# The last two FFN groups of an attention and FFN kernel: Strassen's scheme on fp32 products, or Karatsuba's on 12-bit halves in float32r

## The chip, the core and the metric

The kernel runs on one core of a Trainium2 chip. The time is that of one execution on the device, in microseconds (us). A core has a matrix engine (TensorE, PE in the profile; its weight loads are PEld), a vector engine (VectorE, DVE), a scalar engine (ScalarE, ACT), a general one (GpSimd, POOL) and a queue for transfers (SyncE, SP). The kernel's matmuls write to PSUM, in tiles of 128 x 512 fp32 that it calls banks; the other operands lie in SBUF.

## What is computed

Threshold attention over 8 sequences of 576 tokens with 8 heads of 64, then an FFN with ELU over the 4608 tokens, all in fp32:

```python
scores = scale * np.matmul(q, k.transpose(0, 1, 3, 2))
thresh = np.max(scores, axis=-1, keepdims=True) - tau
scores = np.where(scores >= thresh, scores, -1000000000.0)
attn = np.exp(scores - max); attn = attn / (sum + 1e-09)     # over the last axis
x = np.matmul(attn, v)                                       # (4608, 512)
h = x @ w_in                                                 # (4608, 2048)
g = np.where(h > 0.0, h, np.exp(np.minimum(h, 0.0)) - 1.0)
out = g @ w_out                                              # (4608, 512)
```

## The kernel before

The FFN works on groups of 512 tokens. Group 0 is done with plain products (`ffn1`, `ffn2_plain`), the others as told here. Group 0 to 7 are the first 512 tokens of each sequence; the 64 tokens left of each sequence make group 8. `xts[g]` holds a group's tokens turned, as four slices `j` of 128 channels; for group 8 they are collected in DRAM (`xtail`) as each sequence is finished, and the part of the last sequence's last head pair comes last.

The attention runs a head pair at a time. From the second sequence on, its steps (`wide_step`, `tail_step`) and the FFN of an earlier sequence share TensorE: after each half step the loop at L1954 lets `ffn_quarters` run a number of quarters of FFN products. The order on each engine is written out: `on_pe` moves a clock by a planned cost for each piece of matmul work, and `at` puts the work of the other engines on an agenda at planned times; the agenda's order is the order in which the engines' queues get their instructions. On the chip the queues run in that order as soon as what each instruction waits for is there.

A group is done by Strassen's scheme with seven products in place of eight. `first_product(g, u)` (L1643) makes one of eight units of the hidden layer: seven products (`left`, `right` at L1660) of two matmuls each with 256 columns, accumulated in three PSUM banks, their sums taken apart by ACT copies, POOL and DVE additions (`after_` at L1720), then exp, minus one and a maximum (`exp`, `minus`, `elu`). `sums` (L1738) makes the sums of the hidden layer that the second product needs; `second_round(g, r)` (L1774) does the output product in two rounds, each with two chunks of 256 tokens, seven products of four matmuls each (L1804). The sums of the weights are made early in the kernel, kept in DRAM (`win_sums`, `wout_sums`) and loaded by SP when they are due (`next_in`, `next_t`); parts of `w_in_sb` and `w_out_sb` in SBUF are replaced by differences (`change_in`, `change_out`).

Groups 1 to 6 run this way between attention steps. After the last attention step (`pr == NP + 1`), where the values of the last head pair are made and copied to `xts[7]`, sums of group 7's tokens are taken (`sums_x`, L1270) and groups 7 and 8 follow with nothing else on TensorE; their order is the list at L2032. The loop at L2005 and L2036 places the remaining sums.

Of the kernel before, what the change touches and what calls it, by code (L numbers as in the profile page):

```python
# [10 lines left out]
FP32 = mybir.dt.float32  # L11
U32 = mybir.dt.uint32
I32 = mybir.dt.int32
AF = mybir.ActivationFunctionType
# [353 lines left out]
def kernel(  # L368
# [33 lines left out]
    raw = ctx.enter_context(tc.tile_pool(name="raw", bufs=1))  # L402
    qkp = ctx.enter_context(tc.tile_pool(name="qkp", bufs=2))
    att = ctx.enter_context(tc.tile_pool(name="att", bufs=2))
    small = ctx.enter_context(tc.tile_pool(name="small", bufs=4))
    wtp = ctx.enter_context(tc.tile_pool(name="wtp", bufs=1))
    xpool = ctx.enter_context(tc.tile_pool(name="xpool", bufs=2))
    gpool = ctx.enter_context(tc.tile_pool(name="gpool", bufs=1))
    epool = ctx.enter_context(tc.tile_pool(name="epool", bufs=1))
# [28 lines left out]
    w_in_sb = const.tile([P, KJ, DF], FP32, name="w_in_sb")  # L438
# [13 lines left out]
    pieces = [(moe_w_in, w_in_sb[:, j, n : n + WN], j, n) for n in range(0, DF, WN) for j in range(KJ)]  # L452
# [86 lines left out]
    def load_v(pr):  # L539
        b, j = divmod(pr, NPAIR)  # L540
        tiles = raws[pr]
        vm = tiles["vm"] = (wstage if pr < 2 else raw).tile([P, 2, NC, D], FP32, name="vm", bufs=2)
# [304 lines left out]
    def turn_squares(pr, i):  # L847
        w = open_steps.pop((pr, i))["w"]
        if late:
            x = late["x"].tile([P, NT, NCH, T], FP32, name="x", bufs=2)  # L850
        else:
            x = wstage.tile([P, 2 * S + TAIL], FP32, name="x", bufs=2)[:, : NT * NCH * T]
            x = x.rearrange("p (g c n) -> p g c n", c=NCH, n=T)
# [189 lines left out]
    def values_out(pr, part, pv):  # L1043
# [5 lines left out]
        if part:  # L1049
            xs = epool.tile([P, TAIL], FP32, name="xs", bufs=2)  # L1050
# [28 lines left out]
    def ffn1(c, u):  # L1079
# [4 lines left out]
        def part(x):  # L1084
# [4 lines left out]
            for j in range(j0, j0 + 2):  # L1089
                nc.tensor.matmul(loc["ph"][:, k], w_in_sb[:, j, ft * P : (ft + 1) * P],  # L1090
# [46 lines left out]
    def ffn2_plain(c, i, part):  # L1137
# [7 lines left out]
        def done():  # L1145
            ot = epool.tile([P, DM], FP32, name="ot", bufs=4)
# [63 lines left out]
    def blocks_in(u):  # L1210
        f0, f1 = (slice(f * P, (f + 1) * P) for f in (u, NU + u))
        return w_in_sb[:, :2, f0], w_in_sb[:, 2:, f0], w_in_sb[:, :2, f1], w_in_sb[:, 2:, f1]

    def room_in(u):
# [3 lines left out]
        sw = late["x"].tile([P, 3, 2, P], FP32, name="sw", bufs=2)  # L1218
# [77 lines left out]
    def early_tasks():  # L1296
# [35 lines left out]
        def leave_early():  # L1332
            early.close()
            late["x"] = wpool[0] = ctx.enter_context(tc.tile_pool(name="late", bufs=1))
# [121 lines left out]
        for n in range(MIDDLE):  # L1456
# [103 lines left out]
            if n >= SWITCH:  # L1560
# [9 lines left out]
                if n >= MIDDLE - 2:  # L1570
                    def some(x):
                        if "jobs" not in late:
                            late["jobs"] = sums_x(1, [late["x"].tile([P, 2, CT], FP32, name=f"x{z}") for z in range(3)])
# [27 lines left out]
    with tc.manual_schedule():  # L1601
# [39 lines left out]
        first_order = [(g, u) for g in range(1, B + 1) for u in range(NU)]  # L1641
# [435 lines left out]
```

## Time and profile before

| | us |
|---|---|
| median of 3 runs | 1278.2 (1277.52 to 1280.78) |
| span of the profiled execution, first to last instruction | 1275.5 |
| of it up to 1055 | 1055.0: PE busy 1045.5, DVE 893.3, ACT 553.0, POOL 697.5 |
| most of group 6's last second round | 1055.0 to 1071.6 |
| the last attention step on TensorE | 1071.6 to 1077.3: PE busy 5.25, DVE 2.65, ACT 1.05, POOL 0 |
| groups 7 and 8 | 1077.3 to 1271.6 |
| the last additions and the store | 1271.6 to 1275.5 |

Of the profiled execution the trace holds the span; it lies 2.7 us under the median. Times in rows of the timeline are us from the start of the span; the first number is the start, the second the length. `x8` stands for eight records in a row. A matmul's length in the trace is modelled and overlaps the next, so its rate is read from starts. A row of a source line gives min, median and max in ns, then the first and last start.

### The profile page before, as it was taken

The page shows a single profiled execution, that of the slowest core. Times are in us where ns is not written, and L with a number is a line of the kernel's source. Part 1 is how long each engine was busy: PE and PEld are TensorE (multiplying, and loading weights), DVE is VectorE, ACT ScalarE, POOL GpSimd, SP SyncE. Part 2 cuts the span into 40 slices and gives each one's busy share as a digit, 9 for nine tenths or more (in the row PEclk, how much of TensorE's full clock was granted, in tenths as well). Part 3 has the DMA queues.
Part 4 walks back from the last instruction along what each step waited for, and adds up shares of the span by engine and source line. Part 5 has one row for each costly group of instructions (what it writes and reads, how often), then busy time and mean ns, then how long its engine had stood idle before and what let it go on. Part 6 is the DMA issues. An engine that isn't in the chain of part 4 may idle for free.

```text
span 1275.5 us, 21472 instructions
## 1 busy us (share of the span) xinstructions
PE 1261.3 (99%) x6726; PEld 983.8 (77%) x6726; DVE 994.8 (78%) x2142; ACT 606.7 (48%) x1309; POOL 789.2 (62%) x1141
## 2 busy tenths in 40 slices
PE   8999999999999999999999999999999999999998
PEld 6675575467778887878888877878887888888887
DVE  7888877888889979898889888988989772544534
ACT  7899776664443535252625353443535251421320
POOL 4778665786585748584766657675757473534533
PEclk9999999999999999999999999999999999999999
DMA  7467688997988998999889998988898874122211
GB/s 141 150 170 190 169 244 236 259 278 200 251 217 241 252 239 228 252 262 229 232 233 269 225 256 205 263 225 243 214 268 232 241 229 177 53 77 73 83 62 34
DMA packets 329586, 258.35 MB, mean 203 GB/s; under 512 B 209536, under 2 KB 290432, under 8 KB 329472
## 3 DMA queue, kind: packets, MB, share of 16 engines
q1 hardware_dynamic: 327376, 256.50, 73.7%
q8 instruction: 53, 0.87, 0.3%
q10 hardware_dynamic: 2096, 0.48, 0.2%
q14 instruction: 61, 0.50, 0.1%
HBM read 167.12 MB, written 89.78 MB: 201 GB/s over the span
## 4 chain that ended last, share of the span: by engine, by line
PE 91%; DVE 3%; DMA 2%; ACT 1%; issue 1%; SPq 1%; POOL 1%; DVEq 0%; ACTq 0%; POOLq 0%
PE f L1804 30%; PE f L1664 29%; PE sc L965 8%; PE sc L1038 7%; PE f L1090 4%; PE sc L661 3%; PE f L1142 3%; PE pv L918 2%; PE rt L780 1%; PE sc L1030 1%; PE sc L1025 1%; DMA there<-x 1%; PE pv L913 1%; DVE x L856 1%; DMA qm<-in_q_dram 0%
## 5 line engine op out<-in xcount | busy, mean ns | idle before, releaser
L972 DVE TENSOR_REDUCE mx<-sc 128x1 f32<-128x576 f32 x207 | 148.2, 750 | 29.5 <-PE sc L965 25.6
L714 POOL TENSOR_SCALAR w<-w,rs 128x576 f32<-128x576 f32 x144 | 115.8, 812 | 70.8 <-DVE rs L777 70.1
L992 ACT ACTIVATE w<-sc,mx 128x576 f32<-128x576 f32 x113 | 81.4, 739 | 115.0 <-DVE mx L972 98.0
L1664 PE MATMUL f<-xt,sw 128*128 128x256 f32 x512 | 124.0, 385 | 1.1 <-ACT g L1726 0.5
L1664 PE MATMUL f<-xt,w_in_sb 128*128 128x256 f32 x512 | 122.2, 381 | 0.5 <-ACT w L1678 0.5
L856 DVE STREAM_TRANSPOSE x<-w 128x512 f32<-128x512 f32 (+1 forms) x153 | 108.9, 744 | 13.0 <-POOL w L714 11.2
L984 POOL TENSOR_SCALAR th<-mx,ntau 128x2 f32<-128x2 f32 (+1 forms) x114 | 33.8, 296 | 133.3 <-DVE mx L972 133.2
L1664 PEld LDWEIGHTS f<-xt,sw 128*128 128x128 f32 x512 | 93.5, 190 | 21.5 <-issue 4.5
L1664 PEld LDWEIGHTS f<-xt,w_in_sb 128*128 128x128 f32 x512 | 96.2, 190 | 16.1 <-ACT w L1678 3.1
L1804 PE MATMUL f<-w_out_sb,g 128*128 128x256 f32 x448 | 107.1, 382 | 0.0
L1804 PE MATMUL f<-w_out_sb,s 128*128 128x256 f32 x448 | 107.0, 382 | 0.0
L1664 PE MATMUL f<-x,w_in_sb 128*128 128x256 f32 x448 | 105.9, 379 | 0.0
L1804 PE MATMUL f<-t,s 128*128 128x256 f32 x448 | 105.8, 379 | 0.0
L965 PE MATMUL sc<-kT,qT 64*128 64x448 f32 (+4 forms) x736 | 102.7, 416 | 0.0
L965 PEld LDWEIGHTS sc<-kT,qT 64*128 64x128 f32 x736 | 80.9, 186 | 24.4 <-issue 16.2
L1751 POOL TENSOR_TENSOR s<-g 128x256 f32<-128x256 f32 x104 | 80.5, 780 | 27.4 <-PE f L1804 20.1
L999 DVE SCALAR_TENSOR_TENSOR w<-sc,th,w 128x576 f32<-128x576 f32 x113 | 88.2, 810 | 9.5 <-ACT w L992 9.2
L1804 PEld LDWEIGHTS f<-w_out_sb,g 128*128 128x128 f32 x448 | 84.1, 190 | 14.2 <-issue 3.2
L1804 PEld LDWEIGHTS f<-w_out_sb,s 128*128 128x128 f32 x448 | 84.1, 190 | 13.6 <-issue 2.5
L1664 PEld LDWEIGHTS f<-x,w_in_sb 128*128 128x128 f32 x448 | 85.0, 190 | 11.8 <-ACT s L1678 0.3
L1804 PEld LDWEIGHTS f<-t,s 128*128 128x128 f32 x448 | 85.1, 190 | 11.6
L714 POOL TENSOR_SCALAR e<-e,rs 128x576 f32<-128x576 f32 x91 | 67.0, 740 | 35.3 <-DVE rs L777 33.9
(233 smaller groups left out, 2858.7 us busy)
## 6 DMA issues: line engine op xcount, KB each, us to landing
there<-x SPq DMA_DIRECT2D x444, 144.0 KB, 3.5
wTb<-there SPq DMA_DIRECT2D x58, 576.0 KB, 6.3
wTa<-there SPq DMA_DIRECT2D x53, 576.0 KB, 4.9
sw<-win_sums SPq DMA_DIRECT2D x62, 384.0 KB, 4.0
t<-wout_sums SPq DMA_DIRECT2D x45, 512.0 KB, 5.5
qm<-in_q_dram SPq DMA_DIRECT2D x124, 72.0 KB, 4.8
wst<-in_moe_w_in_dram SPq DMA_DIRECT2D x16, 512.0 KB, 4.4
vm<-in_v_dram SPq DMA_DIRECT2D x64, 128.0 KB, 3.5
```

Of the source, the lines that this page charges most:

```text
L661: nc.tensor.matmul(scs[h][:, a, :HALF], qs[r], kT[r, k0 : k0 + HALF], start=True, stop=True)
L714: nc.gpsimd.tensor_scalar(wv, wv, st["rs"][:, h : h + 1], 1.0, ALU.mult, ALU.mult)
L856: nc.vector.transpose(x[:, :, c0 : c0 + nc_], src.rearrange("p (c g n) -> p g c n", c=nc_, n=T))
L965: on_banks(nc.tensor.matmul(o, qT[r, i * P : (i + 1) * P], kT[r, k0 : k0 + n], start=True, stop=True, skip_group_check=True), o)
L972: on_banks(nc.vector.tensor_reduce(st["mx"][:, h : h + 1], st["sc", h], axis=AX.XY if i == NC else AX.X, op=ALU.max, negate=True), st["sc" ...
L992: on_banks(nc.scalar.activation(st["e", h], st["sc", h], AF.Exp, bias=st["mx"][:, h : h + 1]), st["sc", h])
L999: on_banks(nc.vector.scalar_tensor_tensor(st["e", h], st["sc", h], st["th"][:, h : h + 1], st["e", h], ALU.is_ge, ALU.mult, accum_out=st[" ...
L1038: on_banks(nc.tensor.matmul(o, vm[:, h, c], parts[part][:, g0:g1, h * (NC + 1) + c], start=False, stop=(c == NC - 1), skip_group_check=Tru ...
L1090: nc.tensor.matmul(loc["ph"][:, k], w_in_sb[:, j, ft * P : (ft + 1) * P], xts[g][:, j, hf * CT : (hf + 1) * CT], start=(j == 0), stop=(j = ...
L1664: nc.tensor.matmul(loc["banks"][place], left[:, j], right[:, j], start=(begins and j == 0), stop=(j == 1), skip_group_check=True)
L1751: engine.tensor_tensor(o, x, y, op)
L1804: nc.tensor.matmul(place(m), lhs, rhs, start=(begins and v == 0), stop=(v == RU - 1), skip_group_check=True)
```

## The change

Up to group 6 every engine's instructions stay as they are, in the same order (some tiles lie elsewhere: pools are opened so that the attention's memory and Strassen's can be given back early; `w_in_sb` becomes two tiles, `w_in_lo` and `w_in_hi`). Groups 7 and 8 are done anew.

Every operand v is cut in two: a = v x (1 - 2^-13), rounded on writing to the 4-byte type float32r, and the rest b = v - a. With a third operand made of both, three products a·a', b·(b' scaled) and a cross product give the whole. For a weight: `weights_cut` (ACT), `weights_rest` (POOL), `weights_scaled` (ACT), `weights_cross` (DVE). For tokens and for the hidden layer: `cut` (ACT), `rest` (DVE or POOL), `cross` (DVE). Each works on 128 x 512. Before weights can be cut, the differences in them are undone (`restore_in` on DVE, `restore_out` on POOL, 256 columns each).

`split_begin` starts this 13 us after the beginning of the step `pr == NP`, while group 6's last second round still runs: it gives back the attention's memory, loads group 8's tokens, and cuts three slices of group 7's tokens, two weight blocks and two slices of group 8. The rest follows in the new stage. First product: 32 units (one block of 128 hidden channels of one group each), of 12 matmuls of 512 columns: the first five are of group 7, then blocks of group 8 and group 7 come mostly in turn; ACT scales the PSUM bank between the first eight and the last four. Second product: for each group 16 blocks, for each block four tiles of 128 tokens with three matmuls of 512 columns. The first three and the last three blocks are ordered by tile, so that these six are wanted together.

```diff
+        def cut(key, src, cols=slice(0, DM), fresh=True):
+            a = take(key, F32R) if fresh else parts[key][0][0]
+            nc.scalar.activation(a[:, cols], src()[:, cols], AF.Copy, scale=CUT)
+        def rest(key, src, engine, cols=slice(0, DM), fresh=True):
+            b = take(key, F32R) if fresh else parts[key][1][0]
+            engine.tensor_tensor(b[:, cols], src()[:, cols], parts[key][0][0].bitcast(FP32)[:, cols], ALU.subtract)
+        def cross(key, src, cols=slice(0, DM), fresh=True):
+            s = take(key, F32R) if fresh else parts[key][2][0]
+            nc.vector.scalar_tensor_tensor(s[:, cols], parts[key][0][0].bitcast(FP32)[:, cols], 1.0 + EPS, src()[:, cols],
+                                           ALU.mult, ALU.subtract)
+        def split_tokens(t, key, src, engine):
+            at(t, lambda: cut(key, src))
+            at(t + 0.8, lambda: rest(key, src, engine))
+            at(t + (0.8 if engine is nc.gpsimd else 1.5), lambda: cross(key, src))
...
+        def weights_rest(key, src, engine):
+            d = slot(FP32)
+            parts["d", key] = [d]
+            engine.tensor_tensor(like(d[0], src()), src(), like(parts[key][0][0].bitcast(FP32), src()), ALU.subtract)
+        def weights_scaled(key):
+            nc.scalar.activation(take(key, F32R), parts["d", key][0][0], AF.Copy, scale=1.0 / EPS)
+        def weights_cross(key):
+            nc.vector.scalar_tensor_tensor(take(key, F32R), parts["d", key][0][0], 1.0 / EPS,
+                                           parts[key][0][0].bitcast(FP32), ALU.mult, ALU.subtract)
+            drop(("d", key))
...
+        def split_weights(t, key, src, engine):
+            at(t, lambda: weights_cut(key, src))
+            at(t + 0.7, lambda: weights_rest(key, src, engine))
+            end = t + (2.3 if engine is nc.gpsimd else 1.6)
+            at(end, lambda: weights_scaled(key))
+            at(end + 0.1, lambda: weights_cross(key))
...
+        def split_begin():
+            t = now[0]
+            attention.close()
+            open_slots("r", 24, "right")
+            xts[B] = xpool.tile([P, KJ, MAIN], FP32, name="xt")
+            nc.sync.dma_start(xts[B][:, : KJ - 1], xtail[: KJ - 1].rearrange("j p n -> p j n"))
+            nc.sync.dma_start(xts[B][:, KJ - 1, : late_columns.start], xtail[KJ - 1, :, : late_columns.start])
+            for j in range(KJ - 1):
+                split_tokens(t + 0.2 + 2.2 * j, ("x", B - 1, j), x_of(B - 1, j), nc.vector)
+            for f in range(2):
+                at(t + 6.6 + 3.0 * f, lambda f=f: restore_in(f))
+                split_weights(t + 7.2 + 3.0 * f, ("in", f), w_in_of(f), nc.gpsimd)
+            for j in range(2):
+                split_tokens(t + 13.0 + 2.4 * j, ("x", B, j), x_of(B, j), nc.vector)
...
+            if pr == NP:
+                at(t + 13.0, split_begin)
...
+        UNIT, ONE = 2.58, 0.215
+        order = [(g7, f) for f in range(5)]
...
+        split_tokens(begin + 1.0, ("x", g8, 2), x_of(g8, 2), nc.gpsimd)
+        split_tokens(begin + 6.0, ("x", g8, last), x_of(g8, last), nc.vector)
+        for f in range(2, NFT):
+            t = max(begin + 1.5 + 2.6 * (f - 2), start_of[g7, f] - 7.0)
+            at(t - 0.6 if f < NU else begin + 2.0 + 2.5 * (f - NU), lambda f=f: restore_in(f))
+            split_weights(t, ("in", f), w_in_of(f), nc.gpsimd)
+        for u in range(NU):
+            at(begin + 30.0 + 5.0 * u, lambda u=u: restore_out(u))
...
+        def first_round(n, js):
+                    nc.tensor.matmul(o, w.rearrange("p (j f) -> p j f", j=KJ)[:, j], m, start=(j == 0 and x == 0),
+                                     stop=(j == KJ - 1 and x == 1), skip_group_check=True)
+        def cross_round(n):
...
+            at(t + 0.05, exp)
+            at(t + 0.85, minus)
+            at(t + 1.65, elu)
...
+        for f in range(NFT):
+            lead = 9.0 - 1.2 * min(f, EDGE - 1) if f < EDGE else 6.5
+            t = start_f(middle, f) - lead + 1.5 * min(f, EDGE) * (f < EDGE)
+            split_weights(t, ("out", f), w_out_of(f), nc.gpsimd)
+            split_g(t + 0.6, g7, f, nc.vector)
+            t = start_f(end, f) - (9.0 if f < EDGE else 6.5) + 1.5 * f * (f < EDGE)
+            at(t + 1.0, lambda f=f: nc.vector.tensor_tensor(take(("cross", f), F32R), parts["out", f][1][0].bitcast(FP32),
+                                                            parts["out", f][0][0].bitcast(FP32), ALU.subtract))
+            split_g(t, g8, f, nc.gpsimd if f % 2 else nc.vector)
+        def second(g, f, i):
+            tok = slice(i * P, (i + 1) * P)
+            for x in range(3):
+                h = issued(("h", g, f), x)
+                w = issued(("out", f), x) if x < 2 or g == g7 else issued(("cross", f), 0)
+                nc.tensor.matmul(banks8[2 * i + x // 2], h[:, tok], w, start=(f == 0 and x != 1),
+                                 stop=(f == NFT - 1 and x != 0), skip_group_check=True)
...
+            if f == NFT - 1:
...
+                    at(t + 0.05 + 0.4 * x, lambda cols=cols: nc.scalar.activation(
+                        o[:, cols], banks8[2 * i][:, cols], AF.Copy, scale=1.0 + EPS))
+                    at(t + (0.5 if done else 0.8) + 0.45 * x, lambda cols=cols: nc.vector.tensor_tensor(
+                        o[:, cols], banks8[2 * i + 1][:, cols], o[:, cols], ALU.add))
```

`EDGE` is 3, `EPS` 2^-12 and `CUT` 1 - 2^-13; `begin`, `middle` and `end` are the planned starts of the stage and of the second products of groups 7 and 8. Slots for the cut operands are two pools of 24 and 34 tiles of 128 x 512.

276 lines of the change are left out of this document (197 added, 79 removed).

## The prediction

> **What bounds the kernel now.** I read the page's totals and its chain of waits first, then the windows, then the order of time on TensorE at the end.
>
> ```profile
> span 1275.5 us, 21472 instructions
> PE 1261.3 (99%) x6726; PEld 983.8 (77%) x6726; DVE 994.8 (78%) x2142; ACT 606.7 (48%) x1309; POOL 789.2 (62%) x1141
> PE 91%; DVE 3%; DMA 2%; ACT 1%; issue 1%; SPq 1%; POOL 1%; DVEq 0%; ACTq 0%; POOLq 0%
> ```
>
> TensorE is busy 99% of the span and 91% of the chain that ended last is TensorE. Nothing else can shorten the kernel but less array work. The instructions of every engine stand in the same order in both programs until the last second round of group 6, so only the end matters; the windows split it (after the length: busy us of PE, PEld, DVE, ACT, POOL).
>
> ```profile
> 1055.00:1071.60 16.60, 16.60 (x78) 14.36 (x76) 3.64 (x9) 0.37 (x1) 9.71 (x14) 1.00 0.28 103
> 1077.30:1174.40 97.10, 97.08 (x450) 85.48 (x451) 51.05 (x88) 29.14 (x69) 43.88 (x58) 1.00 0.23 78
> 1174.40:1271.60 97.20, 96.74 (x448) 84.56 (x446) 43.67 (x82) 23.17 (x55) 38.06 (x51) 1.00 0.20 62
> 1271.60:1275.50 3.90, 0.10 (x1) 0.00 (x0) 0.53 (x2) 0.00 (x0) 0.00 (x0) 0.83 0.30 67
> ```
>
> Groups 7 and 8 fill 1077.3 to 1271.6, TensorE without gaps, the other engines at most half used. The clock is 1.00. The time per instruction comes from starts in the timeline:
>
> ```profile
> 1077.32 1.99 PE L1664 MATMUL f<-xt,sw 128*128 128x256 f32 x8 [0.47 <-ACT xt L1048]
> 1079.15 1.03 PE L1664 MATMUL f<-x,sw 128*128 128x256 f32 x4
> 1080.02 1.89 PE L1664 MATMUL f<-xt,w_in_sb 128*128 128x256 f32 x8
> 1081.74 1.89 PE L1664 MATMUL f<-x,w_in_sb 128*128 128x256 f32 x8
> ...
> 1254.17 1.99 PE L1804 MATMUL f<-w_out_sb,qm 128*128 128x256 f32 x8 [0.46 <-DVE ot L1824]
> 1256.00 1.89 PE L1804 MATMUL f<-w_out_sb,wTa 128*128 128x256 f32 x8
> ...
> 1269.81 1.89 PE L1804 MATMUL f<-w_out_sb,x 128*128 128x256 f32 x8
> L1804 PEld LDWEIGHTS f<-w_out_sb,g 128*128 128x128 f32 x448 | 84.1, 190 | 14.2 <-issue 3.2
> ```
>
> From 1256.00 to 1269.81 are eight rows of x8, 64 records in 13.81 us: 0.2158 each. An fp32 matmul of the program leaves two records (a product of four matmuls shows as x8): 0.4316 us for 256 columns. The weight load of 190 ns hides under each record. 448 matmuls of the two groups are 896 records, 193.4 us; with the waits of 0.47 and 0.46 that is the stage.
>
> **The array work.** The new scheme has 2 groups x (16 blocks x 12 + 16 blocks x 4 token tiles x 3) = 768 matmuls of 512 columns in float32r. No row shows this type. In fp32 256 columns cost four passes of 0.108 us; if one-pass means what it says, 512 columns cost 0.2158, and the 190 ns load still fits under it. For the bound from above, fp32 records of 512 columns:
>
> ```profile
> L1142 PE MATMUL f<-w_out_sb,g 128*128 128x512 f32 x128 | 60.1, 602 | 0.0
> ```
>
> They last 602 ns where those of 256 columns in the page's list last 379 to 385: a record streams 256 columns in 0.22, so one record of 512 would take 0.43. From below, a matmul bound by its weight load would take 0.19. I take 0.2158, as a single pass is what the type is for and two would be odd with both halves gone: 768 x 0.2158 = 165.7, minus 27.7 us. The Trainium skill (FP8 and Floating Point Precision, TensorE Precision Notes) tells of a reduced mode that reads 4-byte values and truncates them, against four passes for true fp32, and names no rate; no run here shows it. The skill's TensorE: Matmul & The Clock Gate (Wait — 56ns, not 53.3ns?) has 215.7 ns for a one-pass matmul of 512 columns in bf16, which would make 165.7 as well. The two old waits go too (minus 0.9).
>
> **What it adds.** Every operand is now cut on chip: ACT cuts, POOL or DVE subtracts, ACT or DVE makes the third operand. Their prices:
>
> ```profile
> L1273 DVE TENSOR_TENSOR x<-xt x19: 672/681/710, 258.1 to 1077.3; 128x512 f32<-128x512 f32 x19
> L1751 DVE TENSOR_TENSOR s<-s,g x8: 415/422/426, 1094.4 to 1212.1; 128x256 f32<-128x256 f32 x8
> L1255 POOL TENSOR_TENSOR t<-w_out_sb x4: 1262/1270/1273, 209.0 to 232.4; 128x512 f32<-128x512 f32 x4
> L1234 POOL TENSOR_TENSOR w_in_sb<-w_in_sb x8: 726/730/1177, 239.1 to 260.5; 128x256 f32<-128x256 f32 x8
> L1704 POOL TENSOR_SCALAR ge<-ge x54: 612/618/831, 273.3 to 1248.3; 128x512 f32<-128x512 f32 x54
> L1694 ACT ACTIVATE ge<-g x77: 612/630/636, 272.3 to 1198.5; 128x512 f32<-128x512 f32 x77
> L1097 ACT ACTIVATE g<-f x16: 574/590/599, 60.7 to 207.8; 128x512 f32<-128x512 f32 x16
> L1104 DVE SCALAR_TENSOR_TENSOR g<-g,f x13: 667/680/689, 63.5 to 209.1; 128x512 f32<-128x512 f32 x13
> L1714 DVE SCALAR_TENSOR_TENSOR g<-ge,g x77: 660/771/1208, 274.6 to 1199.9; 128x512 f32<-128x512 f32 x77
> ```
>
> So 512 columns cost 0.68 on DVE, 1.27 on POOL (subtract) or 0.62 (scalar), 0.63 on ACT; a restore of 256 columns 0.42 on DVE, 0.73 on POOL. Alone each engine has room in 2.58 us, TensorE's time for one block (12 x 0.2158 = 2.59): in group 7's second product DVE needs 3 x 0.68 = 2.04, POOL 1.27, ACT 3 x 0.63 = 1.89; in the first product ACT has scale and exp 2 x 0.59 and two weight steps 2 x 0.63 = 2.44 in the first five units. But the maximum of L1714, 1208 ns, shows that they are not alone:
>
> ```profile
> 1104.31 0.72 POOL L1683 TENSOR_TENSOR u<-u,w 128x256 f32<-128x256 f32 x1
> 1104.37 1.21 DVE L1714 SCALAR_TENSOR_TENSOR g<-ge,g 128x512 f32<-128x512 f32 x1 [0.51 <-POOL ge L1704]
> 1105.11 1.06 POOL L1683 TENSOR_TENSOR s<-s,u 128x256 f32<-128x256 f32 x1
> 1109.39 0.61 POOL L1704 TENSOR_SCALAR ge<-ge 128x512 f32<-128x512 f32 x1
> 1109.45 1.08 DVE L1714 SCALAR_TENSOR_TENSOR wTb<-km,wTb 128x512 f32<-128x512 f32 x1 [0.51 <-POOL km L1704]
> ```
>
> DVE ends 0.55 after POOL's end at 1105.03, POOL's next then 0.59 after DVE's at 1105.58; at 1110.00 the same, 0.53. An instruction of DVE with two SBUF inputs and one of POOL run in turn; a waiting one hides some 0.13 of its own time. L1104, with one input in PSUM, never stretches. Every split on DVE has two SBUF inputs, so DVE and POOL times **add**. Three places follow, each bounded by full prices and by prices less 0.13.
>
> *Before the stage* (1055 to 1071.6, 16.6 us): POOL has 9.7 already; the change puts in five token splits (10 x 0.68), two weight blocks (2 x 1.27 + 2 x 0.68) and two restores (2 x 0.42): 21.2, 4.6 too much; with 0.13 off each of 30 instructions, 17.3, 0.7 too much. The second block's subtract stands on POOL ahead of the sums of chunk 1 that TensorE needs
>
> ```profile
> 1064.35 1.41 POOL L1751 TENSOR_TENSOR s<-g 128x256 f32<-128x256 f32 x2
> 1066.36 1.89 PE L1804 MATMUL f<-t,s 128*128 128x256 f32 x8
> ```
>
> only 0.6 us after they are made, and waits itself for DVE's restore and ACT's cut. So I take 3.5.
>
> *The start of the first product*: five units of group 7 come in a row, each with a new weight block. Until TensorE wants block 4 (4 x 2.58 = 10.3 us) the pair has: POOL four subtracts (5.1) and two scalars (1.2); DVE four half splits (1.7), three splits of group 8 (2.0), two weight crosses (1.4), seven restores (2.9): 14.3, 4.0 over; less 0.13 for each of 22, 11.4, 1.1 over. Queues here mix restores for later blocks ahead of what is urgent: 3.5. Later blocks come every second unit (5.2 us). The other 27 units, 69.7 us of matmuls, hide what the pair still has (27 scalars, 11 subtracts, 12 crosses, 7 restores on DVE and 8 on POOL: 48 us): nothing, and at most those 48 without the cover.
>
> *Group 7's second product*: a block costs the pair 1.27 + 3 x 0.68 = 3.31 against 2.58. From the first subtract, 8.3 us ahead of the product by the queue's plan, to the last three blocks, wanted together 33.5 us into it, are 41.8 us; 16 blocks and three scalars are 54.9, 13.1 over; less 0.13 for each of 67, 46.2, 4.4 over. As the two engines wait for each other all the time here, the low end is nearer: 6. Group 8 reuses the weights: 0.68 + 0.68 and 0.68 or 1.27 are 2.34 a block on average, 37 us under 41 of matmuls: nothing (the 37 would show if DVE started late). ACT's share is hidden everywhere by those same matmuls; its thinnest cover is 0.14 us a unit, in the first five.
>
> The Trainium skill (SBUF — State Buffer, Who interferes with whom) says that these two kinds of instruction exclude each other for a whole instruction; it speaks against this change. By that rule to the letter the three waits are the upper ends, 4.6, 4.0 and 13.1, and the time 1271.8; the rows above agree but for the 0.13 that overlap.
>
> *The end*: the last tile needs ACT's scale (0.37 for half) ahead of DVE's add: +0.5 (0 to 1). The loads of Strassen's sums go and two loads of tokens come; TensorE waits for no DMA in this stage (share 0.20 to 0.28), so both at nothing.
>
> Sum: -27.7 - 0.9 + 3.5 + 3.5 + 6 + 0.5 = -15.1. The profiled span of 1275.5 lies 2.7 under the median of 1278.2, and that stays around it: 1260.4 of span, **1263 us**. With the lower ends of the waits (0.7, 1.1, 4.4, 0) 1255.8, with the upper ones 1272.3.
>
> **Rivals.** (1) The pair's blocking costs nothing, since queues run ahead; for it: POOL was 39 to 45% busy here; against: 1208 ns at L1714. What is left is the chain: a subtract of 1.27 and a sum of 0.72 against 0.6 of slack, 1.4, and as much at the start: -28.6 + 2.8 + 0.5, 1253. (2) The pair is worse than full prices, as no instruction arrives in time and each restarts a chain cut, subtract, scale (0.63 + 1.27 + 0.63): another 3 to 6 on the upper ends, 1275 to 1278. (3) float32r is not one-pass but streams like one fp32 record, 0.43: 768 x 0.43 = 330, plus 137, all splits hidden: 1414, **slower**; it decides from 0.25 us a matmul. Against it: nothing would be gained by the type. (4) In group 7's second product weight and token chains run one block at a time, for want of slots: cut, subtract, scale, cross 3.2 and token 2.0 make 5.2 a block, (5.2 - 2.58) x 16 = 42 in place of 6: 1299, slower; it decides from 3.8 a block. Against it: 58 slots of 512 columns stand open.
>
> **Chances.** Forecast (1256 to 1272) 0.62; (1) 0.10; (2) 0.15; (3) 0.06; (4) 0.05; the rest 0.02. A measurement of this kernel tells 0.3%, some 3.8 us, from no change: (2) lies half there. Faster 0.82, same 0.06, slower 0.12. The range of 1253 to 1277 leaves out 0.2.
>
> **What would show it.** The new profile should have about 768 matmul records starting 0.216 apart; DVE groups at the subtract and cross lines with means well over 0.68 and POOL subtracts over 1.27; gaps on TensorE released by POOL ahead of the stage, by ACT in the first 13 us of it, by DVE in group 7's second product and none in group 8's. Matmuls 0.43 apart, or means at 0.68 beside gaps, would make it wrong.

## The result, and the profile after

| | before | after |
|---|---|---|
| median | 1278.2 us (9 runs, 1277.05 to 1280.78) | 1274.72 us (9 runs, 1273.13 to 1276.79) |
| span of the profiled execution | 1275.5 | 1271.7 |

The ratio is 0.9969, 95% interval 0.9959 to 0.9979: faster by 3.5 us, where 15 were forecast. The time lies above the upper end of the range, 1272. The page of the changed kernel, totals and chain of waits:

```profile
span 1271.7 us, 21210 instructions
PE 1246.8 (98%) x6598; PEld 957.3 (75%) x6598; DVE 1035.4 (81%) x2146; ACT 651.2 (51%) x1363; POOL 804.6 (63%) x1114
PE 87%; DVE 5%; issue 2%; DMA 2%; ACT 2%; POOL 1%; SPq 1%; ACTq 0%; DVEq 0%; POOLq 0%
```

TensorE still bounds it. It is busy 14.5 us less than before, but its share of the chain falls from 91% to 87%: there are waits now. The windows of the changed kernel (after the length: PE, PEld, DVE, ACT, POOL, then the clock and the DMA share):

```profile
1048.24:1077.19 28.95, 25.72 (x114) 20.70 (x112) 15.42 (x24) 6.25 (x12) 17.78 (x19) 1.00 0.42 148
...
1098.26:1173.51 75.25, 75.25 (x334) 62.33 (x332) 33.62 (x50) 46.82 (x87) 42.84 (x50) 1.00 0.00 1
1173.51:1217.00 43.49, 40.31 (x168) 32.18 (x167) 43.49 (x50) 24.54 (x44) 25.80 (x16) 0.96 0.00 1
...
1210.60:1217.00 6.40, 3.93 (x11) 2.81 (x10) 6.40 (x12) 2.18 (x4) 2.19 (x1) 0.73 0.00 0
...
1213.51:1216.92 3.41, 3.41 (x8) 2.74 (x9) 3.41 (x6) 1.66 (x3) 2.11 (x1) 0.50 0.00 0
...
1217.00:1266.88 49.88, 49.88 (x219) 40.71 (x217) 34.57 (x44) 10.59 (x20) 13.47 (x8) 1.00 0.10 32
```

Group 6's last second round takes 28.95 and has gaps; the first product after its fifth unit and group 8's second product have none; in group 7's second product DVE is busy for every one of 43.49 us and TensorE is not. The rate and the gaps are in the timeline:

```profile
1068.39 0.41 DVE L2055 TENSOR_TENSOR w_in_lo<-w_in_lo,w_in_hi 128x256 f32<-128x256 f32 x1
1068.84 0.63 ACT L2021 ACTIVATE r<-w_in_lo 128x512 fp32r<-128x512 f32 x1 [0.94 <-DVE w_in_lo L2055]
1069.55 1.26 POOL L2026 TENSOR_TENSOR r<-w_in_lo,r 128x512 f32<-128x512 f32 x1 [1.62 <-ACT r L2021]
1070.77 1.86 POOL L1762 TENSOR_TENSOR s<-g 128x256 f32<-128x256 f32 x2
1071.55 2.26 PE L1815 MATMUL f<-t,s 128*128 128x256 f32 x8 [2.88 <-POOL s L1762]
...
1083.88 1.35 POOL L2001 TENSOR_TENSOR l<-xt,l 128x512 fp32r<-128x512 f32 x1 [7.08 <-ACT l L1997]
1085.19 1.47 POOL L2026 TENSOR_TENSOR l<-w_in_lo,l 128x512 f32<-128x512 f32 x1
1086.14 0.39 PE L2182 MATMUL f<-r,l 128*128 128x512 f32 x1
1086.86 0.63 ACT L2029 ACTIVATE l<-l 128x512 fp32r<-128x512 f32 x1
1087.54 1.88 PE L2182 MATMUL f<-r,l 128*128 128x512 f32 x7 [1.01 <-ACT l L2029]
...
1098.26 1.07 PE L2182 MATMUL f<-r,r 128*128 128x512 f32 x4
1099.16 1.07 PE L2182 MATMUL f<-l,r 128*128 128x512 f32 x4
1100.07 1.07 PE L2195 MATMUL f<-r,l 128*128 128x512 f32 x4
...
1190.34 0.39 PE L2261 MATMUL f<-w_in_hi,l 128*128 128x512 f32 x1
...
1191.04 0.39 PE L2261 MATMUL f<-w_in_hi,r 128*128 128x512 f32 x1
...
1195.28 0.68 DVE L2001 TENSOR_TENSOR r<-w_in_lo,l 128x512 fp32r<-128x512 f32 x1
1195.89 0.68 DVE L2005 SCALAR_TENSOR_TENSOR r<-l,w_in_lo 128x512 fp32r<-128x512 f32 x1
1196.08 1.64 POOL L2026 TENSOR_TENSOR l<-w_out_sb,w_in_hi 128x512 f32<-128x512 f32 x1 [1.27 <-ACT w_in_hi L2021]
1196.49 1.78 DVE L2032 SCALAR_TENSOR_TENSOR r<-r,w_in_hi 128x512 fp32r<-128x512 f32 x1
1198.19 0.68 DVE L2001 TENSOR_TENSOR r<-w_in_lo,r 128x512 fp32r<-128x512 f32 x1
...
1213.46 0.78 PE L2261 MATMUL f<-r,l 128*128 128x512 f32 x1 [2.47 <-DVE r L2032]
1214.04 0.63 PE L2261 MATMUL f<-r,r 128*128 128x512 f32 x1
```

Four things are to be seen. (a) 1098.26 to 1100.07 are eight matmuls in 1.81 us: 0.2267 each, not 0.2158; 1190.34 to 1191.04, where every third streams `w_in_hi`, are three in 0.70 (two rows between are left out): 0.231 to 0.233. (b) The 2.88 us ahead of the stage wait for a sum on POOL, behind the subtract of 1069.55, which waited for a cut on ACT, which waited for a restore on DVE. (c) At the start of the first product TensorE waits for ACT's scaled weights, three times about alike. (d) DVE needs 1195.28 to 1198.19, 2.91 us, for each block of group 7's second product, of which the weight cross takes 1.70, since POOL's subtract runs in between; at 1213.46 TensorE has waited 2.47 us, and the matmuls behind it start 0.43 to 0.58 apart: the clock granted was half for 3.41 us (0.50 in the window from 1213.51, 0.73 on average in the one from 1210.60).

A step is the time from the start of one matmul to the start of the next. With the starts of the first matmuls of each stretch in both traces, the 3.8 us of span come out like this:

| term | forecast | measured | how |
|---|---|---|---|
| all up to group 6's last second round | 0 | +1.0 | its first matmul at 1047.26 and 1048.24; 0.85 of it is there from 258 us on, for a reason that was not traced |
| that round | +3.5 | +4.6 | 24.37 and 28.95 from its first matmul to the attention step's |
| array work | -27.7 | -18.2 | 193.4, and 175.2 = stage of 184.5 less its waits of 9.35 (next three rows) |
| waits at the start | +3.5 | +4.0 | steps over 0.26 between starts, up to 1096, less 0.2267 each |
| waits in group 7's second product | +6 | +3.6 | the same at 1175.1 and 1210.6 |
| matmuls at half clock behind the gap | - | +1.7 | eight steps, 1213.46 to 1217.0, in 3.53 |
| old waits | -0.9 | -1.4 | 0.83 in the old stage, 0.54 ahead of it |
| end, behind the last matmul | +0.5 | +0.9 | 3.96 and 4.86 |
| sum | -15.1 | -3.8 | |

768 matmuls in 175.2 us are 0.2281 each. That one term holds 9.5 of the 11.3 us by which the sum is off.

### The profile page after: what moved, and what is told of

It is laid out like the page before. It is cut to its first block, busy times and chain, and to the rows that moved or that the text cites. A ratio compares the mean times of both kernels' runs of the same rounds, so it can differ in the third digit from the quotient of the medians.

```text
span 1271.7 us, 21210 instructions
## 1 busy us (share of the span) xinstructions
PE 1246.8 (98%) x6598; PEld 957.3 (75%) x6598; DVE 1035.4 (81%) x2146; ACT 651.2 (51%) x1363; POOL 804.6 (63%) x1114
## 4 chain that ended last, share of the span: by engine, by line
PE 87%; DVE 5%; issue 2%; DMA 2%; ACT 2%; POOL 1%; SPq 1%; ACTq 0%; DVEq 0%; POOLq 0%
PE f L1815 22%; PE f L1675 22%; PE sc L974 8%; PE sc L1047 7%; PE f L2182 4%; PE f L1099 4%; PE f L2261 4%; PE sc L670 3%; PE f L1151 3%; PE pv L927 2%; PE f L2195 2%; PE rt L789 1%; PE sc L1039 1%; PE sc L1034 1%; DMA there<-x 1%
## 5 line engine op out<-in xcount | busy, mean ns | idle before, releaser
L981 DVE TENSOR_REDUCE mx<-sc 128x1 f32<-128x576 f32 x207 | 148.3, 750 | 29.2 <-PE sc L974 25.2
L865 DVE STREAM_TRANSPOSE x<-w 128x512 f32<-128x512 f32 (+1 forms) x153 | 108.9, 744 | 14.0 <-POOL w L723 11.3
L1815 PE MATMUL f<-t,s 128*128 128x256 f32 x384 | 91.7, 380 | 3.2 <-POOL s L1762 3.1
L1675 PE MATMUL f<-xt,sw 128*128 128x256 f32 x384 | 93.6, 386 | 0.7 <-ACT g L1737 0.5
L1815 PE MATMUL f<-w_out_sb,g 128*128 128x256 f32 x384 | 92.0, 382 | 0.0
L1815 PE MATMUL f<-w_out_sb,s 128*128 128x256 f32 x384 | 91.9, 382 | 0.0
L1815 PEld LDWEIGHTS f<-t,s 128*128 128x128 f32 x384 | 72.5, 190 | 14.9 <-POOL s L1762 5.2
L1675 PEld LDWEIGHTS f<-xt,sw 128*128 128x128 f32 x384 | 69.3, 189 | 17.3 <-issue 5.0
L1001 ACT ACTIVATE e<-sc,mx 128x576 f32<-128x576 f32 x91 | 66.5, 744 | 24.6 <-DVE mx L981 23.2
L1008 DVE SCALAR_TENSOR_TENSOR e<-sc,th,e 128x576 f32<-128x576 f32 x91 | 71.2, 810 | 7.6 <-ACT e L1001 7.6
L865 DVE STREAM_TRANSPOSE x<-e 128x640 f32<-128x640 f32 x92 | 66.0, 755 | 1.0
L727 DVE TENSOR_REDUCE mx<-sc 128x1 f32<-128x576 f32 x81 | 59.3, 747 | 5.5 <-PE sc L670 5.1
```

What stands on the lines that cost most here:

```text
L727: nc.vector.tensor_reduce(st["mx"][:, h : h + 1], st[h][:, :, :HALF], axis=AX.XY, op=ALU.max, negate=True)
L865: nc.vector.transpose(x[:, :, c0 : c0 + nc_], src.rearrange("p (c g n) -> p g c n", c=nc_, n=T))
L981: on_banks(nc.vector.tensor_reduce(st["mx"][:, h : h + 1], st["sc", h], axis=AX.XY if i == NC else AX.X, op=ALU.max, negate=True), st["sc" ...
L1001: on_banks(nc.scalar.activation(st["e", h], st["sc", h], AF.Exp, bias=st["mx"][:, h : h + 1]), st["sc", h])
L1008: on_banks(nc.vector.scalar_tensor_tensor(st["e", h], st["sc", h], st["th"][:, h : h + 1], st["e", h], ALU.is_ge, ALU.mult, accum_out=st[" ...
L1675: nc.tensor.matmul(loc["banks"][place], left[:, j], right[:, j], start=(begins and j == 0), stop=(j == 1), skip_group_check=True)
```

## The experiments

Differences are to the changed kernel's 1274.72 unless said otherwise; ratios are to the kernel before, measured beside it.

**What a float32r matmul costs.** Behind the last store, rows of 16 matmuls on idle engines (`w` and `m` lie like the slots, `hi` is `w_in_hi`, `half` bf16, `full` fp32):

```diff
         until(1e9)
+        hi = parts["c"][0]
...
+        kinds = (lambda k: (cut4(w, k), m), lambda k: (w[:, :P], m), lambda k: (cut4(w, k, 64), m),
+                 lambda k: (cut4(w, k, 32), m), lambda k: (cut4(w, k, 32), m[:, :384]), lambda k: (cut4(w, k, 32), m[:, :CT]),
+                 lambda k: (cut4(w, k), m[:, :CT]), lambda k: (cut4(half[1], k), half[0]),
+                 lambda k: (cut4(full, k), full[:, :CT]), lambda k: (cut4(w, k), hi[:, 1]),
...
+                nc.tensor.matmul(o[: st.shape[1], : mv.shape[1]], st, mv, start=k == 0, stop=k == 15, skip_group_check=True)
```

> After the last store the changed kernel is followed by 19 rows of 16 matmuls each on otherwise idle engines, so only the rows' spacing matters, not the time. In the stage float32r matmuls of 512 columns start 0.2267 us apart, and 0.231 apart while a slice of w_in_hi streams, where fp32 records start 0.2158 apart. Theory A (a fixed extra of some 0.011 per float32r matmul, whatever its widths): 512 columns stay at 0.227 with 128, 64 or 32 stationary columns; with 32 stationary columns 384 columns take 0.173 and 256 columns 0.119. Theory B (the 4-byte weight load of 0.19 isn't wholly hidden): 0.227 with 128 stationary columns falls to 0.216 with 64 and 32; 256 columns with 128 stationary ones stay near 0.2. Theory C (the moving operand streams a sixteenth slower): 0.227 for any stationary width, 384 columns 0.170, 256 columns 0.113. Theory D (the other engines disturb it): 0.216 in the first row, since nothing else runs. The same stationary block sixteen times: 0.227 for A and C; for B as well, unless a repeated load is left out. bf16 of 512 columns and fp32 records of 256: 0.216 for all. For w_in_hi (it lies elsewhere in SBUF than the slots, and on a multiple of 64 bytes, the slots 32 off): if place or alignment decides, 0.23 or more for rows that stream w_in_hi, and, if alignment, for the row that starts 32 bytes into a slot as well.

Windows of this run, TensorE alone, each from the first start of a kind to that of the next. In order: 64 and 32 stationary columns; 32 with 384 and with 256 moving columns; bf16 (15 recorded); fp32 of 256 columns (31 steps); the moving operand 0 and 32 bytes into a slot; both operands in `w_in_hi`; moving in a slot, stationary in `w_in_hi`:

```profile
1279.38:1283.05 3.67, 3.67 (x17) 1.00 0.00 0
1283.05:1286.76 3.71, 3.71 (x17) 1.00 0.00 0
1286.76:1289.54 2.78, 2.78 (x18) 1.00 0.00 0
1289.54:1291.42 1.88, 1.88 (x17) 1.00 0.00 0
...
1293.57:1296.81 3.24, 3.24 (x16) 1.00 0.00 0
1296.81:1303.50 6.69, 6.69 (x32) 1.00 0.01 2
1314.85:1318.48 3.63, 3.63 (x18) 1.00 0.00 0
...
1322.19:1325.92 3.73, 3.73 (x17) 1.00 0.00 0
...
1329.59:1333.24 3.65, 3.65 (x17) 1.00 0.00 0
1333.24:1336.98 3.74, 3.74 (x18) 1.00 0.00 0
```

Divided by 16: 0.229 and 0.232 with narrow weights, so the weight load isn't it (B); 0.174 for 384 and 0.1175 for 256 columns, which is 0.162 and 0.108 (512 columns of 0.2158, in proportion) plus 0.012 and 0.010: a fixed extra (A), and no slower streaming, which would give 0.170 and 0.113 (C); with 128 stationary columns 256 columns take 0.120, 0.012 over too. A expected 0.227 with narrow weights too; that they come out 0.002 to 0.005 above it is not explained. The other engines are idle here, so they aren't it (D). bf16 at 3.24 / 15 and fp32 at 6.69 / 31 keep 0.216: the extra belongs to float32r. Place matters too: 0.2267 where both operands lie alike, 0.234 for one in `w_in_hi` and one in a slot, but 0.2267 again (the last steps of that row) with both in `w_in_hi`, and 0.233 for 32 bytes into a slot. It is their difference that costs.

**Equal remainders, first try.** In the compiled program `w_in_hi` starts at a remainder of 64 by 128 bytes, the slots at 96. A pad ahead of each pool of slots makes all 64:

```diff
+            pad = split_stack.enter_context(tc.tile_pool(name=name + "_pad", bufs=1, side=side))
+            pad.tile([P, 8 if name == "r" else 24], FP32, name=name + "_pad")
             pool = split_stack.enter_context(tc.tile_pool(name=name, bufs=1, side=side, reuse_waits="tile"))
```

> Changed kernel, with a pad of 32 and of 96 bytes ahead of the two pools of slots, so that slots and w_in_hi start at the same remainder by 128 bytes. Theory A (a float32r matmul costs 0.227 where both operands start at the same remainder, 0.231 to 0.234 where not, and in the second products every third matmul streams w_in_hi): all undisturbed matmuls of both second products start 0.2267 apart, the mean outside the waits falls from 0.2282 to 0.227, 0.9 us less of stage. Theory B (w_in_hi is slower for its place in SBUF): 0.231 stays and so does the stage. The time of one look can't tell 0.9 us.

A miss for both: the mean step outside the waits rose from 0.2282 to 0.2316, and in the first product alone from 0.2270 to 0.2317. By 256 bytes the two pools now stood at 192 and 64, where they had been 224 both. So 128 is the wrong measure.

**By offset.** Rows of 24, the moving operand off by a number of bytes:

```diff
+        for b in (0, 4, 8, 12, 16, 24, 32, 40, 48, 64, 80, 96, 112, 128, 256, 512):
+            rows(w, m, 0, b)
```

> Again rows of matmuls behind the changed kernel, 24 each, on idle engines: float32r of 512 columns with the moving operand 0, 16, 32, 48, 64, 96, 128, 160, 192, 256, 320, 384, 448, 512, 1024 and 2048 bytes off the stationary one's remainder by 512; then both shifted by 32 bytes, both by 256, the stationary one 512 and the moving one 256 on; then bf16 and fp32 with the operands 0 and 32 bytes apart. So far: 0.2267 apart at equal remainders, 0.2294 to 0.2335 at 16 to 160 bytes of difference, and 0.231 in the run with slots at remainders of 448 and 64 by 512. Theory A (equal remainders by 512 bytes cost the fixed extra of 0.011 alone, others 0.003 to 0.007 more; the extra itself isn't a matter of place): 0.2267 for 0, 512, 1024, 2048 and for both shifted, more for all others, none under 0.2265. Theory B (the extra is itself a clash of the streamed operand with the next weight load, which some difference avoids): a row at 0.216. For bf16 and fp32 records 0.216 with equal remainders; at 32 bytes apart 0.216 if the clash belongs to float32r, more if it doesn't.

Windows of this run, 24 steps each: 32 bytes off, 160, 256, 512, and bf16 32 bytes off:

```profile
1284.45:1290.04 5.59, 5.59 (x25) 1.00 0.00 0
1312.36:1317.98 5.62, 5.62 (x25) 1.00 0.00 0
1323.58:1329.05 5.47, 5.47 (x26) 1.00 0.00 0
1345.74:1351.19 5.45, 5.45 (x26) 1.00 0.00 0
...
1383.63:1388.81 5.18, 5.18 (x26) 1.00 0.00 0
```

0.233, 0.234, 0.228, 0.227 and 0.216. The measure is 256 bytes: 256, 512, 1024 and 2048 all have 0.227 to 0.228; 64 and 320 have 0.229 to 0.230, 128 and 384 0.233, 192 and 448 0.233. No row of float32r is under 0.2265, so none of the differences tried avoids the extra; bf16 and fp32 stay at 0.216 with 32 bytes between. Theory A held but for its 512.

**Equal remainders, in the kernel.** Pads of 160 and 352 bytes in the same two lines (40 and 88 columns in place of 8 and 24):

> Changed kernel, with pads of 160 and 352 bytes, so that slots and w_in_hi have the same remainder by 512 bytes (320). Theory A (equal remainders by 512 decide): all undisturbed matmuls of the stage start 0.2267 apart, stage 0.9 to 1.1 shorter than the changed kernel's 184.5 for equal waits. Theory B (it is something else in the place, such as the remainder of 480 of the slots as they were): 0.231 as with the pads of 32 and 96 bytes.

The mean step outside the waits is 0.2269 in place of 0.2282. The stage, 183.99, is 0.5 shorter, its waits 0.4 longer. It is a single execution, 1273.76, which can't tell half a us. So of the 9.4 us by which the array work exceeds its 165.7, 8.4 are the fixed extra (768 x 0.0109) and about 1 the remainders.

**The forecast's rate, put in.** First by bf16 views of the tiles, every second 2-byte element, so that the splits stay and the products keep only the upper halves:

```diff
+        def as_half(t):
+            return t.bitcast(mybir.dt.bfloat16).rearrange("p (n a) -> p n a", a=2)[:, :, 1]
```

> Changed kernel in which the 768 matmuls read their operands through bf16 views of the same tiles (the upper two bytes of each value, so the products keep some 8 bits and the last parts of the halves are left out); all splits on ACT, POOL and DVE are as they were. bf16 rows of 512 columns ran 0.2158 apart; that these read every second 2-byte element isn't measured yet. Theory A (only the rate of the array work was mis-sized and the waits of the forecast hold at its rate): matmuls 0.2158 apart, 165.7, the waits at the start some 4, in group 7's second product 5 to 6 in place of 3.6, since DVE's 2.91 a block now stands against 2.59: stage 175 to 176 in place of 184.5, 1265 to 1267. Theory B (the waits were small only because the array was slow: at 2.59 a block the pair costs its full price, 13.1): stage 183 or more, 1273 or more. If the views stream slower than 0.2158, neither is told apart and only the spacing counts.

The views ran 0.225 apart: inconclusive for the waits. The time is 1272.41 (ratio 0.9956, 0.994 to 0.9973), the gap in group 7's second product 3.50 from start to start where it was 2.86. Then with the operands written as bf16 in a row:

```diff
-            return pool.tile([P, DM], dt, name=name), home
+            t = pool.tile([P, DM], FP32, name=name)
+            return t if dt is FP32 else t.bitcast(BF16)[:, :DM], home
```

> Changed kernel with the cut operands written as bf16, 512 in a row, in the front half of the same tiles (the halves then keep 8 bits each in place of 12, so the products are less exact; the number of instructions and matmuls is the same). Contiguous bf16 rows ran 0.2158 apart, views with a step of two 0.225. Theory A (only the rate was mis-sized, the waits of the forecast hold at its rate): 165.7 of matmuls, waits of some 4 at the start and 5 to 6 in group 7's second product, 2.91 a block on DVE against 2.59: stage 175 to 176 in place of 184.5, 1265 to 1267, or 1.7 more where the half clock follows a gap. Theory B (at 2.59 a block the pair's full price shows, 13.1): stage 183 or more, 1273 or more. If DVE or POOL take another time with bf16 than 0.68 and 1.27, the waits move with them and the rows tell by how much.

Timeline and the window of group 7's second product of this run, which begins the stage at 1086.75 (the profile is of its slowest execution, 1269.07; the median is 1265.43):

```profile
1104.27 1.03 PE L2184 MATMUL f<-r,r 128*128 128x512 bf16 x4
1105.13 1.03 PE L2184 MATMUL f<-l,r 128*128 128x512 bf16 x4
1105.99 1.03 PE L2197 MATMUL f<-r,l 128*128 128x512 bf16 x4
...
1194.52 1.50 POOL L2028 TENSOR_TENSOR l<-w_out_sb,w_in_hi 128x512 f32<-128x512 f32 x1 [1.26 <-ACT w_in_hi L2023]
...
1197.28 1.51 POOL L2028 TENSOR_TENSOR r<-w_out_sb,l 128x512 f32<-128x512 f32 x1 [1.26 <-ACT l L2023]
```

```profile
1174.80:1217.00 42.20, 38.08 (x165) 16.83 (x168) 42.20 (x52) 23.40 (x43) 23.96 (x15) 0.96 0.00 1
```

Eight matmuls in 1.72: 0.215. From 1086.75 to the end of the last matmul at 1262.13 are 175.4 us; the forecast's terms for the stage make 165.7 + 3.5 + 6 = 175.2. The time is 1265.43 (ratio 0.9889, 0.9872 to 0.9907), 9.3 under the changed kernel, which is the size of the array term's error. DVE is again busy throughout group 7's second product. So the rate is what the forecast missed (theory A). The waits match it less well: of the 9.6 us that aren't array work, 3.7 are waits at the start, 4.2 waits in group 7's second product, where 5 to 6 were expected, and 1.7 half clock behind the gap, which the forecast had not. That they add up to its 9.5 is partly luck. The tiles also changed the pair's price a little: from one of POOL's subtracts to the next, a block, are 2.76 us here and 2.91 in the changed kernel.

**The wait ahead of the stage.** The second weight block behind group 6's last sums:

```diff
-                at(t + 6.6 + 3.0 * f, lambda f=f: restore_in(f))
-                split_weights(t + 7.2 + 3.0 * f, ("in", f), w_in_of(f), nc.gpsimd)
+                at(t + 6.6 + 1.0 * f, lambda f=f: restore_in(f))
+                split_weights(t + 7.2 + 9.0 * f, ("in", f), w_in_of(f), nc.gpsimd)
```

> Changed kernel, with the second weight block's split planned 6 us later in split_begin and its restore 2 us earlier, so that its subtract stands behind group 6's last sums on POOL. Theory A (the gap of 3.26 between matmul starts ahead of the last but two products is the queue order on POOL: the subtract of 1.26 and its wait of 1.62 for DVE's restore and ACT's cut stand ahead of the sums): the gap falls to about 0.7 and the whole is 2.6 us faster than the changed kernel, 1272.1. Theory B (POOL and DVE have more work than time there, 21 us in 16.6): the gap moves behind, to the chunk's last products or to block 1 at the start of the first product, and the time stays within 1 us of 1274.7.

The row that waited 2.88 us is, in this run:

```profile
1069.06 1.99 PE L1815 MATMUL f<-t,s 128*128 128x256 f32 x8 [0.44 <-POOL s L1762]
```

The time is 1270.62 (ratio 0.9937, 0.9924 to 0.995). The round takes 26.24 in place of 28.95, the step of 3.26 is 0.82, and the three waits at the start are as before: queue order, not too much work, made most of the wait. Smaller steps over the usual, 1.9 us of the 4.6, stay. Of the 4.1 us of the medians that explains 2.7; its profile has no half clock, the changed kernel's lost 1.7 to one.

**The start of the first product.** Blocks 2 and 3 ahead of the stage, two token slices of group 8 behind its start:

```diff
-            for j in range(2):
-                split_tokens(t + 13.0 + 2.4 * j, ("x", B, j), x_of(B, j), nc.vector)
+            for f in range(2, 4):
+                at(t + 14.0 + 3.0 * (f - 2), lambda f=f: restore_in(f))
+                split_weights(t + 20.0 + 3.0 * (f - 2), ("in", f), w_in_of(f), nc.gpsimd)
...
-        split_tokens(begin + 1.0, ("x", g8, 2), x_of(g8, 2), nc.gpsimd)
+        for j in range(2):
+            split_tokens(begin + 2.0 + 2.4 * j, ("x", B, j), x_of(B, j), nc.vector)
+        split_tokens(begin + 7.5, ("x", g8, 2), x_of(g8, 2), nc.gpsimd)
...
-        for f in range(2, NFT):
-            t = max(begin + 1.5 + 2.6 * (f - 2), start_of[g7, f] - 7.0)
+        for f in range(4, NFT):
+            t = max(begin + 1.5 + 2.6 * (f - 4), start_of[g7, f] - 7.0)
```

> Changed kernel, with the weight blocks 2 and 3 split ahead of the stage, where POOL is idle for 7 us, and the first two token slices of group 8 split after its start in their place (the slots are the same 24); block 4 and later are planned earlier. Theory A (the three waits of 1.4 to 1.5 at the start of the first product are single weight chains begun too late, cut, subtract, scale one behind the other, with the token split of group 8 ahead of block 2's subtract on POOL): all three go, 3.8 us off the stage, 1270.9. Theory B (DVE and POOL have more work than time there, 14.3 us in 10.3): the work is the same and only changes places, the waits come back at the first units of group 8; within 1 us of 1274.7.

The window of this run over the first product:

```profile
1083.85:1172.61 88.76, 88.76 (x394) 73.50 (x392) 50.06 (x74) 57.53 (x108) 51.99 (x57) 1.00 0.01 1
```

The time is 1270.98 (ratio 0.9942, 0.9928 to 0.9955), 3.7 faster. Of the steps over 0.26 only the very first, 0.34, is left in the first product; the stage is 180.6. The work is the same and the waits are gone: they were late chains.

**Group 7's second product.** Once the subtracts on DVE (the helper then plans scale and cross 0.7 us earlier), and once the order by block to the end:

```diff
-            split_weights(t, ("out", f), w_out_of(f), nc.gpsimd)
+            split_weights(t, ("out", f), w_out_of(f), nc.vector)
```

> Changed kernel, with the 16 subtracts of the output weights (weights_rest) on DVE in place of POOL. Theory A (DVE's two-input instructions and POOL's exclude each other, so the pair needs 2.91 us a block in group 7's second product, the 1.70 of each weight cross among them, against 2.77 of matmuls): alone on DVE four instructions of 0.60 make 2.41 a block, the crosses fall from 1.78 to 0.68, TensorE's gap of 2.86 at 1210.6 goes and the half clock of 3.4 us behind it: 4.4 us faster than the changed kernel, 1270.3. Theory B (the two engines really share the work, and DVE is the full one): with 16 more subtracts of 0.68 on DVE, 4 x 0.68 = 2.72 a block plus the group 8 work that follows, the gaps grow: 1 to 5 us slower, 1276 to 1280.

```diff
-                     edge + [(f, i) for f in range(EDGE, NFT - EDGE) for i in range(4)] +
-                     [(NFT - EDGE + f, i) for f, i in edge]]
+                     edge + [(f, i) for f in range(EDGE, late) for i in range(4)] +
+                     [(late + f, i) for f, i in edge if late < NFT]]
```

(`late` is NFT for group 7, and `start_f` plans its blocks accordingly.)

> Changed kernel, with group 7's second product kept in order of blocks to its end (its last three blocks are no longer ordered by tile), and its splits planned so. Theory A (the gap of 2.86 comes because three blocks are wanted at once and DVE does their three subtracts, three token crosses and three weight crosses in that order, the last weight crosses at the end): the gap goes, 3 to 4.4 us faster than the changed kernel, 1270.3 to 1271.7. Theory B (the pair is simply too slow, 2.91 a block against 2.77): the lag of 16 x 0.14 = 2.2 us stays whatever the order, and the gap stays at 2 or more; within 1 us of 1274.7.

With the subtracts on DVE 1268.64 (ratio 0.9927, 0.9913 to 0.994), 6.1 faster; the stage 179.2, 5.3 shorter, no gap in the second product. The same work in the timeline of that run:

```profile
1195.03 0.69 DVE L2026 TENSOR_TENSOR r<-w_out_sb,w_in_hi 128x512 f32<-128x512 f32 x1
1195.63 0.69 DVE L2001 TENSOR_TENSOR l<-w_in_lo,r 128x512 fp32r<-128x512 f32 x1
1196.24 0.69 DVE L2032 SCALAR_TENSOR_TENSOR l<-r,w_in_hi 128x512 fp32r<-128x512 f32 x1
1196.84 0.69 DVE L2005 SCALAR_TENSOR_TENSOR l<-r,w_in_lo 128x512 fp32r<-128x512 f32 x1
```

Four instructions in 2.41 us (the next begins at 1197.44) where three took 2.91: the cross falls from 1.78 to 0.69 as soon as POOL doesn't run beside it. By order of blocks it is 1273.2 (0.9959, 0.9946 to 0.9972), 1.5 less than the changed kernel, but the two intervals overlap, so a gain isn't shown; its profile has no half clock behind the gap, which cost 1.7 in the changed kernel's. A gap of 2.18 stays: it is the pair's rate, and the order takes 0.7 off it.

**Four edits together**: the second weight block later, blocks 2 and 3 early, the output subtracts on DVE, and pads, once the first and once the second:

> The output weights' subtracts on DVE, the second weight block's split behind group 6's last sums, blocks 2 and 3 early and the pads, all in one. If the four are independent and the only waits left are those behind group 6's sums (some 1.2 us): stage 768 x 0.2267 = 174.1 and no wait, 28.95 - 2.7 of round ahead of it, the whole 2.7 + 3.8 + 5.3 + 0.9 = 12.7 less than the changed kernel's profiled 1271.7, 1259.0 of span, and 1260 to 1263 as the median. If DVE is then too full, with the subtracts on it: gaps released by DVE in group 7's second product, 1264 to 1268.

> All four edits in one, with these pads in place of those of 32 and 96 bytes, which made the mean 0.2312. If equal remainders by 512 decide: 768 x 0.2267 = 174.1 of stage, 3.5 less than with the other pads, 1260.2 as the median; if not, the same 1263.7 as with the other pads, within 1 us.

With the first pads 1263.74 (ratio 0.9891, 0.9877 to 0.9904), the mean step 0.2312; with the second 1260.92 (ratio **0.9865**, 0.9848 to 0.9881), 0.2267. The window of the latter over group 7's second product:

```profile
1171.00:1215.00 44.00, 44.00 (x196) 36.44 (x195) 41.82 (x68) 27.01 (x49) 8.37 (x4) 1.00 0.07 25
```

TensorE has no idle time there, DVE 2 of 44 us; the stage is 174.3, of which 768 x 0.2267 are 174.1. This version beats both kernels: 17 us under the one before, 13.8 under the changed one.

## Why the forecast was wrong, step by step

The step that failed is one sentence on the array work: "I take 0.2158, as a single pass is what the type is for". It is a single pass, but it costs 0.2267 where both operands start at the same remainder by 256 bytes and 0.229 to 0.2345 elsewhere, 0.2281 on average: 175.2 in place of 165.7. That the load of 190 ns fits under it was right: in the rows behind the kernel, matmuls of 256 columns with full weights start 0.120 apart. The Trainium skill's TensorE: Matmul & The Clock Gate (Wait — 56ns, not 53.3ns?) has 215.7 ns for bf16, and the bf16 rows here agree at 0.216; to carry the rate of another type over to float32r, which no row showed, was the mistake, and the bounds of 0.19 and 0.43 beside it never entered the range with a weight. With bf16 in the tiles, at 0.216, the array work was 165.7 and the time 1265.43, inside the range.

The waits were forecast at 13.0 for the stage and the round ahead of it, and came to 12.2, with 1.7 of half clock on top. **Ahead of the stage** place and queue were right; 4.6 is the upper end of a sum of work, and 2.7 of it went with the queue's order, so the match is luck. **At the start** the size was right (4.0 for 3.5), but not the sum of DVE's and POOL's work behind it: with the same work earlier the waits vanish, so this too is luck. The sentence on queues that mix what is urgent with what isn't was the better one. **Group 7's second product** had the right engine and the right cause; a block costs the pair 2.91 and not 3.31: instructions on DVE start 0.60 apart where the rows' lengths of 0.68 were added, which is 0.24 of it, and the other 0.16 overlap with POOL's subtract (1.27 + 3 x 0.60 less 2.91). The slow matmuls hid some as well, since a block of TensorE took 2.77 and not 2.59. So 3.6 in place of 6. The Trainium skill's SBUF — State Buffer (Who interferes with whom) spoke of this exclusion, and the weight cross of 1.78 beside POOL and 0.69 without it agrees. The upper ends that the prediction took from full prices, 4.6, 4.0 and 13.1, were met in size by the first two places and missed by the third. **Group 8** had no wait, as forecast. **The end** was 0.9, inside its bounds.

Of the rivals, (1) fell with the waits. (2) named the time, 1275, but by restarting chains that cost 3 to 6 more; only one of three places went beyond its forecast by more than 1, so the time came out there by another way. (3) had the right suspect and the wrong size: 0.2281, under the 0.25 from which it would have decided. (4) didn't occur: blocks follow each other at 2.91.

## What to carry to other kernels

A gain that is a count times a rate is worth no more than the rate: where no row shows the type, five hundredths of a rate can be two thirds of the gain, so give the rate a band of its own. Before an idle engine is given work, look whether the busy one must stand still meanwhile: here three instructions beside POOL (2.91 us) took longer than four without it (2.41). A stall at the start of a stage may be work begun too late rather than too much of it; an idle stretch just ahead of it tells which.

## What the runs showed of the hardware that was not expected

A float32r matmul with operands at equal remainders costs 0.010 to 0.016 us more than its columns' share of 0.2158 per 512, over 256, 384 and 512 columns and 32, 64 and 128 stationary ones; 0.011 with 512 and 128. What causes the extra was not found. With 512 and 128 it costs 0.002 to 0.008 more still if its two operands start at different remainders by 256 bytes; bf16 and fp32 at 32 bytes apart don't mind. bf16 with a step of two elements ran 0.225 apart, in a row 0.216.

Behind steps of 2.7 to 3.5 us between matmuls ahead of the stage and in it, the granted clock fell to half for 3.4 us in 10 of 19 cases over the profiles of the changed kernel and of the experiments, and cost some 1.4 to 1.7 us (in the changed kernel's, the window from 1213.51). The same step ahead of the stage, 3.25 to 3.26, did it in some executions and not in others; in the changed kernel's own it didn't. The Trainium skill's TensorE: Matmul & The Clock Gate (Part 1: The HAM clock gate) tells of free-running windows of 3413 ns, an idle one of which brings half clock; the stretches here are 3.41 us long and come by chance, which agrees, but steps under 3.4 us sufficed. So a gap of that size costs up to 1.7 more than its length, and part of the scatter between runs may be this; that part was not tested.
